# Routed attention with a spectral gate behind it: first row sum in thirds, 64-column similarity and sum products, three-bank transposes, and the first head pair routed first

## The chip, the core and the metric

The kernel runs on one core of a Trainium2 chip. The metric is device time in microseconds, the time of one execution. A profile shows each engine of the core: PE (TensorE, matrix products and transposes), DVE (VectorE), ACT (ScalarE), POOL (GpSimd) and SP (SyncE, which issues transfers). The times of the kernel before are 387.03, 386.67 and 388.61 us; their median is 387.03 us.

## What is computed

The first half is attention with a mask from clusters; q, k and v are (4 batches, 8 heads, 768 positions, 64), and there are 16 centroids for each head. The second half is a projection, a circular convolution along the positions, a gate and an output projection.

```python
q_assign = np.argmax(np.einsum('bhsd,hcd->bhsc', q_n, c_n), axis=-1)      # k_assign likewise
mask = q_assign[:, :, :, None] == k_assign[:, :, None, :]
scores = np.where(mask, scale * np.matmul(q, k.transpose(0, 1, 3, 2)), -1000000000.0)
attn = np.exp(scores - np.max(scores, axis=-1, keepdims=True))
attn = attn / (np.sum(attn, axis=-1, keepdims=True) + 1e-09)              # x = attn @ v
x1, x2, x3 = (proj[..., :D], proj[..., D:2 * D], proj[..., 2 * D:])       # proj = x @ w_proj
x2_conv = np.fft.irfft(np.fft.rfft(x2, n=S, axis=1) * H, n=S, axis=1)     # H = rfft(filter_fft)
y = (x1 * x2_conv * x3) @ w_out
```

## The kernel before

**Pairs and groups.** Two heads make a pair, two pairs a group; there are 16 pairs in 8 groups (n = 0 to 7), and two groups make a batch. A pair goes through six key tiles of 128 positions (sk = 0 to 5). For each key tile there are three score products (L660), three exponentials of 128x512 on ACT (L669, L672), the product of the exponentials with v (L683, 8 recorded matmuls, called "pv" here), and the running sum of the exponentials over the key tiles on DVE (L697): one addition of 128x1536 for each key tile but the first two, which share one (`acc<-p,p`). The sums are later added over the partitions, either by a product with ones on PE (L711; groups 0, 1 and 7) or by transfers that accumulate (L731, issued by POOL; the other groups).

**Routing.** For a group, q and k of both pairs are transposed on PE (L556, for groups 0 and 1 L566), copied out of PSUM by ACT or DVE (L261, L263), multiplied with the normalised centroids (`cbd`) to similarities (L586, for group 0 L477), copied, transposed back (L599), and on DVE the position of the largest of 16 is found and made into mask rows (L607 to L624). A transfer transposes these (L629) and small transfers put 16 mask rows beside each head's q and k (L462), so that the score product adds the mask. The similarity product puts four results of 32 rows each into one bank, each by a product that is 32 columns wide; so does the product with ones.

**Gate.** For every batch, `hyena` computes the projections, the transform, the product with the filter's transform and the way back on PE (L74, L809, L451), with its elementwise work on DVE (L822 to L911). It needs tables of sines (`angles`, L337, with the sine function on ACT) and the filter's transform (`tables`, L375), which the kernel works out once at the start.

**Order of the work.** The kernel writes its instructions in an order that a planner works out (`Plan.place`, L113). Every piece of work is an `op` with a cost for each engine that may do it, a due time, and the buffers it reads and writes. The planner fills the engines' queues by readiness and due time; `NUDGE` shifts single due times, and on PE an op that keeps the array's width (`MODES`, L46) is preferred. Each engine then runs its queue strictly in order. PSUM has six banks for scores and other products (0 to 3, 6, 7) and two for the results of the pv product (4, 5). All of group 0 is routed in the order pair 0, pair 1 while the sines and the tables are worked out between; scores of the first pair follow.

The width of a product counts in what follows. Products whose results are 64 (or 32) rows tall are put two (or four) beside each other on the array; this is the similarity product of a group before:

```python
for z in range(4):
    T.nc.tensor.matmul(bank(h.ids[ch])[64 * (z % 2) + 32 * (z // 2):][:32, :384], T.cbd[:, 2 * g + z // 2],
                       T.qkT[z][:, ch], start=True, stop=True)
```

Of the kernel before, what the change touches and what calls it, by code (L numbers as in the profile page):

```python
# [34 lines left out]
ROWS = 16  # L35
LEAD = 2.99901
FIRST = 2
BUSY = 8.09741
HELD = 4
EARLY = 8.73655  # L40
NUDGE = {6:-0.2,9:0.7,10:3.7,11:-0.3,71:-0.3,75:-1.5,90:7.4,91:7.4,129:-0.8,140:0.4,152:2.6,155:-6.2,156:6.6,158:-2.3,167:0.6,169:-4.1,187:-5.6,193:0.1,204:0.1,207:-0.7,209:0.8,212:-0.2,216:15.5,218:8.0,222:-3.8,228:-3.1,238:-1.7,239:-1.7,240:-1.7,243:1.1,245:-2.9,253:-4.1,255:-7.1,256:-7.1,257:-3.0,264:4.3,274:2.3,281:0.9,288:9.1,289:11.6,298:0.6,322:-4.8,328:-9.2,329:-0.5,343:0.7,363:0.5,368:-1.5,369:-1.5,370:0.7,371:-1.5,375:0.1,378:0.5,379:0.7,390:-1.8,391:-0.1,400:-0.2,406:2.8,409:-4.8,410:0.5,416:0.2,418:-1.0,433:-11.9,434:0.6,440:-3.7,479:0.8,480:-0.3,481:-0.5,485:1.1,494:-0.6,495:-4.2,504:2.3,508:-1.9,511:-0.2,517:-0.3,518:-5.0,523:-0.4,524:0.5,526:2.1,539:-2.3,547:0.2,554:10.5,558:0.3,565:-0.3,568:1.6,573:0.4,587:-4.9,590:0.2,595:-17.3,597:-2.4,617:0.7,620:-1.0,631:0.3,634:2.8,646:0.7,658:0.8,664:0.1,665:-1.9,684:2.2,690:-8.8,693:2.2,698:0.1,703:-7.8,704:-1.7,705:-1.7,729:0.5,740:1.0,750:-0.6,759:0.5,767:0.4,779:-0.7,782:1.7,784:-0.1,788:0.7,789:-0.3,790:0.8,800:2.5,805:-3.5,810:1.5,822:0.1,824:0.1,826:-0.5,828:-0.3,843:-8.5,848:-1.7,861:0.5,870:2.5,871:2.5,872:-1.3,883:-5.3,888:-3.6,897:-0.8,898:-1.1,901:-3.5,915:-3.1,926:4.0,936:-4.1,937:-3.0,940:2.9,941:0.4,947:-0.4,949:-0.6,969:-0.8,981:1.0,996:2.0,997:2.0,999:-0.3,1026:2.7,1029:-2.1,1031:0.1,1036:3.2,1039:2.0,1043:-1.2,1048:1.2,1050:-0.1,1054:-1.5,1056:10.8,1062:0.4,1066:0.9,1077:-7.7,1083:-3.4,1092:-0.1,1098:-1.0,1101:0.3,1116:-6.9,1118:-4.2,1122:2.8,1123:2.4,1124:2.4,1127:1.5,1130:-1.5,1131:0.3,1132:-2.9,1143:-2.6,1150:4.6,1157:-0.6,1194:-0.9,1236:-2.9,1253:-0.5,1255:0.7,1257:0.7,1263:0.3,1270:-0.2,1271:-1.1,1276:-3.6,1285:2.1,1286:4.6,1295:4.9,1311:-2.5,1317:-2.0,1321:0.4,1322:0.7,1332:-1.9,1337:-0.6,1351:5.6,1357:0.2,1359:0.5,1363:-0.5,1373:-1.5,1374:1.1,1381:0.2,1383:-0.3,1414:-2.7,1419:-0.5,1422:0.3,1425:0.7,1441:9.4,1450:3.5,1461:2.0,1478:-1.3,1479:3.3,1500:1.2,1501:-8.3,1521:0.2,1529:0.8,1546:0.2,1551:-0.2,1552:-1.1,1555:1.4,1557:0.1,1563:-0.6,1591:0.2,1600:-0.4,1619:-4.8,1624:2.8,1630:-1.5,1634:0.3,1640:-4.0,1641:-4.0,1642:-13.7,1643:-4.0,1655:-4.1,1657:0.4,1666:0.5,1672:1.9,1677:-0.3,1680:2.8,1681:2.8,1682:2.8,1685:-2.9,1697:-0.5,1713:-7.0,1741:5.6,1747:13.3,1764:1.1,1771:-3.3,1774:3.4,1776:0.2,1788:-7.8,1797:0.1,1808:-0.1,1809:-0.1,1814:-4.0,1817:-2.0,1823:3.3,1827:-0.7,1841:-1.3,1844:0.9,1859:2.4,1862:2.5,1863:2.1,1865:-0.3,1870:-0.4,1887:2.4,1890:3.2,1898:-7.4,1901:-0.8,1902:-1.5,1903:-0.8,1904:-0.8,1905:-1.8,1906:-1.8}
# [4 lines left out]
MODES = {"pv": 64, "bc": 64, "half": 64, "sim": 32, "den": 32, "score": 0, "proj": 0, "inv": 0}  # L46
# [30 lines left out]
class Plan:  # L77
# [6 lines left out]
    def op(self, eng, fn, due, r=(), w=(), alloc=None, free=(), lock=False, byts=0, after=(), kind=None, lat=0.0):  # L84
# [3 lines left out]
        o.seq = len(self.ops)  # L88
        o.due += NUDGE.get(o.seq, 0.0)
# [23 lines left out]
    def place(self, free0, banks_for, switch=0.1, wait=0.1, rate=215e3, bonus=10.84378, margin=0.02195, shape=1.63806):  # L113
# [130 lines left out]
def build(T):  # L244
# [3 lines left out]
    T0 = 20.38450  # L248
    TAU1 = 2.97769
    TAU2 = 3.43320  # L250
    NE = 28
# [26 lines left out]

    def dma(e):
        return (T.nc.scalar if e == "ACT" else T.nc.sync).dma_start  # L280
# [10 lines left out]
    def load_qk(n, pr, j, due, after=()):  # L291
        s = qslot[n, pr, j] = len(loads) % NQK
        loads.append(1)

        return [op({"SP": .8, "ACT": .8} if n == 0 else ("SP", .8), lambda e, hp=hp: dma(e)(
            T.qkraw[s][:, :, hp], (T.q, T.k)[j][n // 2, 4 * (n % 2) + 2 * pr + hp].rearrange(
                "(p t) d -> p t d", t=NT)), due, w=[("qkraw", s, hp)], byts=196e3, kind="load", after=after, lat=.5)
            for hp in range(2)]
# [8 lines left out]
    def centroids():  # L307
# [7 lines left out]
        sq = op(("ACT", 1.5), lambda e: T.nc.scalar.activation(cen.s0, cen.ss, Act.Sqrt), 2.4, r=["ss"], w=["s0"])  # L315
# [13 lines left out]
        def cbd(e):  # L329
            cv = ap(h)[:D, :128].rearrange("d (r e c) -> d r e c", r=4, e=2)  # L330
            V().tensor_copy(T.cbd[:D, :, :NC], cv[:, :, 0])
            V().tensor_copy(T.cbd[D:, :, NC:], cv[:, :, 1])
        op(("DVE", .45), cbd, 2.7, r=[h, "cbd0"], w=["cbd"], free=[h])
        return sq


    def angles(sq):  # L337
        sins = []
        MAGIC = 12582912.0
        sc = 2.0 * math.pi / S  # L340
        for m in range(3):
            lo = 256 * (m // 2)
            n, r = (lambda x=x, m=m, lo=lo: x()[m % 2][:, :, lo:lo + 192] for x in (lambda: T.tm, lambda: T.ob))
            nk, rk = ("tm", m % 2, "a", m), ("ob", m % 2, "a", m)
            kc = lambda: T.kc
            due = 1.9 + .8 * m
# [190 lines left out]
    def routing(n):  # L537
# [39 lines left out]
        if n == 0:  # L577
            return got + first_masks(1)
# [597 lines left out]
```

## Time and profile before

| what | value |
|---|---|
| median of the three times | 387.03 us |
| span of the profiled execution, first to last instruction | 385.4 us |
| first transpose on PE; first score product; first exponential | 5.1; 21.7; 22.4 us |
| ACT copies the first pair's result out (L701) | 42.7 us |
| last exponential starts; last matmul ends | 336.4; 381.0 us |
| exponentials 128x512 on ACT, 288 | 0.61 us each |
| running sum 128x1536 on DVE, 80 | 1.75 us each |
| transfers of 64, 32 and 16 rows that accumulate (L731), 30 | issued by POOL, 0.79 us each |

The profiled execution has no other time of its own than its span; the median of the times is 1.6 us above it, and this is taken for what lies around the span. Busy time of an engine is the time in which at least one of its instructions is recorded. A matmul's record holds its way through the array, so that records of successive matmuls overlap, and their number and mean length do not give the time they need together; the chain of waits, which goes from one start to the next, does.

### The profile page before, as it was taken

How to read it: one execution, taken by the hardware profiler on the slowest of the kernel's cores; microseconds unless marked ns; L12 is line 12 of the kernel's file. 1: busy time of each engine (PE TensorE's matmuls, PEld its weight loads, DVE VectorE, ACT ScalarE, POOL GpSimd, SP SyncE). 2: the span in 40 equal slices, each digit the busy share in tenths (PEclk: the TensorE clock that was granted, in tenths of full speed). 3: DMA queues.
4: the chain of work that ended last, by engine and by line, in shares of the span. 5: the costliest groups of instructions: out<-in, count | busy, mean ns of one | idle time of the engine just before them, and what ended most of it. 6: DMA issues, size and time to landing. Idle time of an engine off the chain costs nothing.

```text
span 385.4 us, 8486 instructions
## 1 busy us (share of the span) xinstructions
PE 367.3 (95%) x3262; PEld 207.6 (54%) x3267; DVE 352.3 (91%) x504; ACT 273.1 (71%) x519; POOL 46.6 (12%) x92
## 2 busy tenths in 40 slices
PE   2999899999999999989999999999999999999995
PEld 1564345445655555556555555555455566555682
DVE  8898988998798999998899999999998999999883
ACT  5897987887894979577975967687867367532342
POOL 8602000000012010101010100101010100000400
PEclk9999999999999999999999999999999999999999
DMA  9819984730679669767886896645657551010214
GB/s 176 196 52 216 215 182 120 170 72 22 166 146 187 119 119 143 121 113 126 161 104 174 144 246 108 119 88 91 102 102 198 62 115 43 4 43 2 101 67 163
DMA packets 93860, 47.17 MB, mean 122 GB/s; under 512 B 82088, under 2 KB 87676, under 8 KB 93820
## 3 DMA queue, kind: packets, MB, share of 16 engines
q1 hardware_dynamic: 87836, 36.84, 42.5%
q0 software_dynamic: 2704, 8.98, 16.0%
q10 hardware_dynamic: 3280, 0.82, 1.2%
q8 instruction: 25, 0.41, 0.5%
q14 instruction: 15, 0.12, 0.1%
HBM read 31.59 MB, written 7.40 MB: 101 GB/s over the span
## 4 chain that ended last, share of the span: by engine, by line
PE 65%; DVE 19%; ACT 6%; issue 4%; DMA 3%; SPq 1%; POOL 0%; DVEq 0%; ACTq 0%; POOLq 0%
PE bank L74 24%; PE pair L683 21%; DVE acc L697 6%; PE bank L809 5%; PE bank L72 4%; PE bank L556 3%; ACT p L672 2%; PE bank L586 2%; DMA dr<-dn 2%; DMA aug<-ohT 2%; ACT aug L261 2%; DVE tm L833 2%; PE bank L599 1%; PE bank L451 1%; PE bank L566 1%
## 5 line engine op out<-in xcount | busy, mean ns | idle before, releaser
L683 PE MATMUL pair<-p,vraw 128*64 128x385 f32 x768 | 142.5, 490 | 0.2
L672 ACT ACTIVATE p<-bank 128x512 f32<-128x512 f32 x192 | 113.7, 613 | 34.1 <-PE bank L74 29.3
L697 DVE TENSOR_TENSOR acc<-p,acc 128x1536 f32<-128x1536 f32 x64 | 112.0, 1750 | 3.9 <-ACT p L672 1.5
L683 PEld LDWEIGHTS pair<-p,vraw 128*64 128x64 f32 x768 | 54.2, 136 | 47.8 <-issue 41.1
L74 PE MATMUL bank<-aug,aug 128*64 128x512 bf16 (+3 forms) x580 | 68.4, 328 | 2.1 <-ACT p L672 1.2
L669 ACT ACTIVATE p<-bank 128x512 f32<-128x512 f32 x96 | 58.6, 611 | 6.2 <-PE bank L74 5.6
L74 PEld LDWEIGHTS <-aug 128*64 128x64 bf16 (+1 forms) x580 | 34.4, 109 | 34.5 <-issue 22.4
L731 POOL DMA_DIRECT2D acc<-acc x30 | 23.6, 788 | 242.6 <-DMA acc<-acc 90.3
L74 PE MATMUL bank<-xT,wpj 128*64 128x384 bf16 x440 | 42.7, 326 | 0.0
L261 ACT COPY qkT<-bank 128x384 f32<-128x384 f32 x63 | 28.1, 497 | 10.5 <-PE bank L74 8.9
L74 PEld LDWEIGHTS <-wpj 128*64 128x64 bf16 x440 | 25.5, 109 | 15.9 <-issue 6.4
L697 DVE TENSOR_TENSOR acc<-p,p 128x1536 f32<-128x1536 f32 x16 | 28.0, 1751 | 3.3 <-ACT p L672 3.1
L74 PEld LDWEIGHTS <-y 128*64 128x64 bf16 x464 | 22.9, 110 | 12.6 <-issue 4.4
L261 ACT CAST aug<-qkT 64x768 bf16<-64x768 f32 x33 | 27.3, 829 | 2.5 <-PE bank L74 1.7
L833 DVE TENSOR_TENSOR tm<-bank,hm 128x512 f32<-128x512 f32 x44 | 27.7, 678 | 0.1
L809 PE MATMUL bank<-wpj,xT 128*64 128x512 bf16 x192 | 21.9, 379 | 0.0
L74 PE MATMUL bank<-wout,y 128*64 128x512 bf16 x176 | 21.1, 379 | 0.0
L72 PE MATMUL bank<-aug,aug 80*128 80x256 bf16 (+3 forms) x92 | 20.0, 321 | 0.2
L556 PE MATMUL bank<-ident,qkraw 128*128 128x128 f32 x144 | 19.6, 279 | 0.3 <-DVE sd L898 0.3
L556 PEld LDWEIGHTS bank<-ident,qkraw 128*128 128x128 f32 x144 | 15.6, 140 | 6.9 <-issue 4.5
L261 ACT COPY tm<-bank 128x512 f32<-128x512 f32 x13 | 7.4, 589 | 15.8 <-PE bank L809 12.0
L701 ACT COPY osb<-pair 128x770 f32<-128x770 f32 x16 | 12.9, 809 | 6.9 <-PE pair L683 6.8
(150 smaller groups left out, 433.0 us busy)
## 6 DMA issues: line engine op xcount, KB each, us to landing
vraw<-in_v_dram SPq DMA_DIRECT2D x16, 384.0 KB, 4.3
qkraw<-in_q_dram SPq DMA_DIRECT2D x30, 192.0 KB, 4.1
qkraw<-in_k_dram SPq DMA_DIRECT2D x30, 192.0 KB, 4.1
rb<-dr SPq DMA_DIRECT2D x30, 192.0 KB, 3.7
out_dram<-ob SPq DMA_DIRECT2D x11, 512.0 KB, 3.0
acc<-acc POOLq DMA_DIRECT2D x10, 384.0 KB, 6.2
acc<-acc POOLq DMA_DIRECT2D x10, 192.0 KB, 4.2
y<-in_moe_filter_fft_dram SPq DMA_DIRECT2D x4, 384.0 KB, 7.1
```

The source lines that it names most:

```text
L72: return T.nc.tensor.matmul(out, lhsT, rhs, start=start, stop=stop)
L74: T.nc.tensor.matmul(out[64 * i:64 * i + 64], lhsT[:, 64 * i:64 * i + 64], rhs, start=start, stop=stop)
L261: T.nc.scalar.copy(out, in_)
L556: T.nc.tensor.transpose(bank(h.ids[i // 3])[:, ts(i % 3, 128)], raw(s, i), T.ident)
L669: T.nc.scalar.activation(o, ap(h).rearrange("p (a b) -> p a b", a=2), Act.Exp, scale=0.125)
L672: T.nc.scalar.activation(flat(s)[:, lo:lo + 512], ap(h), Act.Exp, scale=0.125)
L683: T.nc.tensor.matmul(o[64 * hp:64 * hp + 64, ch, :385], T.vraw[vs][:, hp, sk * D:(sk + 1) * D], T.p[slots[sk]][:, hp, 384 * ch:384 * ch + ...
L697: T.nc.vector.tensor_tensor(T.acc[os], P_(t[0]), P_(t[1]) if len(t) == 2 else T.acc[os], op=Alu.add)
L701: op(("ACT", .83), lambda e: T.nc.scalar.copy(T.osb[o3], two(ob)[:, :, :385]), te, r=[ob], w=[("osb", o3)], free=[ob])
L731: op(("POOL", .8), lambda e, rows=rows: T.nc.gpsimd.dma_start(flat_()[:rows], flat_()[rows:2 * rows], accum_op=Alu.add), te, r=[], w=[("ac ...
L809: T.nc.tensor.matmul(ap(h)[64 * i:64 * i + 64], T.xT[xs][:, kt, c:c + 64], T.wpj[:, kt, DM:2 * DM], start=kt == 0, stop=kt == ND - 1)
L833: op(("DVE", .68), lambda e, i=i, cs=cs, r=r, h=h: T.nc.vector.tensor_tensor(T.tm[r][:, cs], ap(h), hmrow(i, (0, 2, 2, 3)[2 * r + cs]), op ...
```

## The change

- **First sum in thirds.** The addition of the first two key tiles (L697, `acc<-p,p`) becomes three additions of 128x512, each of which follows two exponentials and may run on DVE or POOL. In the order of instructions after the change 26 of the 48 thirds are on DVE and 22 on POOL. The later additions are as before.
- **64 columns.** The similarity product and the product with ones use a 64-column operand padded with zeros, and add two products into one 64-row result. The numbers of matmuls stay (8 calls for a group's similarities, 4 for a sum).
- **Three-bank transposes.** From group 2 on, the 12 transposes of a pair's q and k go to three banks, four to a bank, and are copied by three copies of 128x512 in place of four of 128x384.
- **First pair first.** In group 0, q and k of pair 0 are each routed alone and ahead of pair 1; the sines, the tables and the filter's transform come after the first scores. The function tables for square root and exponential are loaded at the start, and the sines run as one block on ACT in the midst of the first pair. The masks of pair 1 in group 0 go by 8 transfers of 16x384.
- **Around it.** Mask rows and small buffers lie in the similarities' buffer (`sim`). All due times (`NUDGE`) are new, and `ONLY` fixes the engine of 194 ops. On PE the changes of the array's width go from 85 to 53, on DVE there are 506 instructions before and 547 after, on ACT 526 and 492, on POOL 97 and 111, on SP 237 and 243.

```diff
-MODES = {"pv": 64, "bc": 64, "half": 64, "sim": 32, "den": 32, "score": 0, "proj": 0, "inv": 0}
+MODES = {"pv": 64, "bc": 64, "half": 64, "sim": 64, "den": 64, "rows": 32, "score": 0, "proj": 0, "inv": 0}
...
-                for z in range(4):
-                    T.nc.tensor.matmul(bank(h.ids[ch])[64 * (z % 2) + 32 * (z // 2):][:32, :384], T.cbd[:, 2 * g + z // 2],
-                                       T.qkT[z][:, ch], start=True, stop=True)
+                for z in (0, 1, 2, 3):
+                    c, j = z // 2, z % 2
+                    T.nc.tensor.matmul(bank(h.ids[ch])[64 * j:64 * j + 64, :384], T.cbd[:, 2 * g + c, 32 - 32 * c:96 - 32 * c],
+                                       T.qkT[z][:, ch], start=c == 0, stop=c == 1)
...
-                        T.nc.tensor.matmul(ap(h)[32 * z:32 * z + 32, :384], T.ones32, T.acc[os][:, hp, ts(ch, 384)],
-                                           start=True, stop=True)
+                        T.nc.tensor.matmul(ap(h)[64 * hp:64 * hp + 64, :384], T.ones[:, 32 - 32 * ch:96 - 32 * ch], T.acc[os][:, hp, ts(ch, 384)],
+                                           start=ch == 0, stop=ch == 1)
...
+                h = Bank(cls, 3)
+                ss = [qslot[n, pr, x] for x in range(2)]
+                def tr2(e, ss=ss, h=h):
+                    for i in range(2 * NT):
+                        T.nc.tensor.transpose(bank(h.ids[i // 4])[:, ts(i % 4, 128)], raw(ss[i // NT], i % NT), T.ident)
+                for c in range(3):
+                    op(EV512, lambda e, pr=pr, c=c, h=h: copy(e, T.qkP[pr][:, ts(c, 512)], bank(h.ids[c])), due + 1.6,
...
+            if sk == 1:
+                for u in range(3):
+                    def part(e, u=u):
...
+                        alu(e).tensor_tensor(o, x, y, op=Alu.add)
+                    op({"DVE": .63, "POOL": 1.33}, part, due - 1 + .2 * u, r=[("p", slots[i], u) for i in range(2)], w=[("acc", os, u)], lock=True)
+            if sk > 1:
...
+                op(("DVE", 1.75), acc, due + 1.1907 - 40 * (last and sk == NT - 1), r=PK(sk), w=AK, lock=True)
...
+    for z in range(2):
+        load_qk(0, 0, z, .3 + z * .1)
+    load_v(0, 0, 8.0)
+    for z in range(2):
+        load_qk(0, 1, z, 6.5 + z * .1)
+    routing(0)
...
+        attention(n, 0)
+        if n == 0:
+            angles()
+            tables()
```

## The prediction

> **What bounds the kernel now.** I read the page's busy shares first, then busy time by stretch (first score at 21.7 us, first pair's result at 42.7, last matmul ended at 381.0), then the chain of waits.
>
> ```profile
> PE 367.3 (95%) x3262; PEld 207.6 (54%) x3267; DVE 352.3 (91%) x504; ACT 273.1 (71%) x519; POOL 46.6 (12%) x92
> ```
>
> PE leads, DVE is close behind. An average does not tell which of them ends; the stretches do (columns: length, then busy us and count of PE, PEld, DVE, ACT, POOL, then clock and DMA):
>
> ```profile
> 0.00:21.70 21.70, 13.88 (x98) 8.62 (x99) 18.59 (x44) 15.41 (x29) 14.46 (x52) 1.00 0.87 183
> 21.70:43.50 21.80, 20.18 (x161) 10.07 (x160) 20.11 (x31) 18.43 (x37) 2.61 (x5) 1.00 0.76 150
> 43.50:340.10 296.60, 293.08 (x2511) 163.12 (x2515) 278.06 (x372) 224.71 (x428) 24.46 (x31) 1.00 0.63 123
> 340.10:381.00 40.90, 40.16 (x499) 25.81 (x493) 35.49 (x60) 13.94 (x28) 5.08 (x4) 1.00 0.15 57
> ```
>
> PE stands idle 7.8 us before the first score, 1.6 in the first pair, and 3.5 + 0.7 = 4.2 in the 337 us after that. From 43.5 us on the kernel is PE's work one after the other, with a last copy and transfer of 4.4 us. So work added to PE adds to the time, work taken from DVE or ACT returns at most the 4.2 us, and only the head has slack.
>
> **The head has one more loss, the clock.** The page's granted clock is 1.00 throughout, but the chain shows the same transposes at two rates: nine in 1.92 us (213 ns each) at the start, twelve in 1.46 (122 ns with the start) later.
>
> ```profile
> 10.63 1.92 PE bank L566 x9
> 12.55 2.69 PE bank L477 x8
> ...
> 57.58 1.46 PE bank L556 x12
> ```
>
> Up to 14.9 us PE ran at half rate. It was busy 7.7 us by then (4.5 + 2.8 + 0.4), about half of that lost. So the head's slack is 7.8 + 1.6 + 3.9 = 13.3 us, of which 5.1 pass before the first load lands: at most 8.2 us can be won.
>
> Beside these rows, the Trainium skill, "TensorE: Matmul & The Clock Gate", section "Part 1: The HAM clock gate", says that the array starts at half rate and is released after about 3.4 us of sustained work, in a free-running window. The trace agrees as far as it goes: bursts at 5.1 and 7.6 us did not release it, unbroken work from 10.2 us did after some 4.7. By that rule a head with fewer matmuls and more waits stays slow longer, some 1 to 3 us by an estimate from these rows; my sum does not use it.
>
> **Wider products: PE, on the path.** The chain gives what a product costs from start to start (start, us, what):
>
> ```profile
> 102.53 1.30 PE pair L683 x8
> 103.82 0.44 PE bank L74 x6
> 104.26 1.43 PE bank L586 x16
> ...
> 61.36 0.78 PE bank L711 x8
> ```
>
> A pv product (L683) is 64 columns wide: 8 records of 385 columns in 1.30 us, 0.162 us a record. The similarities (L586) are 32 wide: 16 records of 384 columns in 1.43 us, 0.09 a record: twice as many lie beside each other. After the change they are as wide as pv, with the same number of calls, neighbours in the order going to opposite halves, so 16 x 0.162 = 2.60 us: +1.17, seven times, +8.2. The sum product (L711) goes from 0.78 to 8 x 0.162 = 1.30: +0.52, six times, +3.1. In group 0 the two similarities of pair 0 stand alone, one half of the array empty: 0.65 us more each at full rate, +1.3.
>
> What this buys is fewer changes of width, 85 to 53. The chain's 1.43 and 0.78 hold one change each; the 26 at both ends of 13 products leave 13 to count. A price: pv pieces followed by transposes take 1.45 us and others 1.29, so at most 0.16; the 16 records of L586 at 0.081 are 1.30, so 0.13. I take 0.10, as 1.43 also holds the fill: -1.3, and -0.4 for the few other changes. Sum on PE: 8.2 + 3.1 + 1.3 - 1.7 = **+10.9 us** (9 to 13). The transposes stay 12 for a pair whether in two banks a tensor or three a pair: 0.
>
> **The head.** Before the first score PE has 0.5 us less to do by the order of instructions (9.6 against 10.1 at full rate: sines' and group 1's transposes out, 1.3 of similarity in). When does that score come? q's transposes start at 5.1 as before; k's second half landed at 7.6, and the first loads still share the queues with pair 1's: 7.2. Six slow transposes 1.3: 8.5. The two similarities, four calls one after another, 2.6 us at full rate and 5.1 at half: I take 4.3, 12.8. Copy 0.47, transposes 0.4, then ten half-sized DVE operations of some 0.28 us (rows of 0.55): 16.5. Mask transposes, pair 1's similarity and transposes, which PE has ahead of the first score, 1.2 beyond what DVE covers; a copy of 16 rows 0.79: 18.5. That is 3.2 us sooner, 2.7 net of the 0.5. In the first pair ACT is next: from the first exponential to the pair's result it has 26 exponentials (15.9), nine copies (4.5), a cast (0.83), the block of sines with two table loads (6.7, from rows of 1.28, 0.52, 0.62, 0.30, 0.19) and four small copies (1.2): 29.1, less 0.09 of overlap for each of 45, 25.0 us. Before it was 42.7 - 22.4 = 20.3. In that stretch PE has 3.6 us more to do by the order of instructions (20.8 against 17.2: some of it was done later before, 1.2 is the wider similarity), so 4.7 - 3.6 = 1.1 are lost. Head: **-1.6 us**. Bounds: -8.2 (all slack) and +3 (the first score no earlier).
>
> **DVE.** Sixteen additions of 1.751 go: -28.0. 26 thirds of about 0.64 (a 128x512 addition stands at 0.679): +16.6. Copies that go from ACT to DVE by the fixed engines and 512-wide copies: about +15. Net **+3.5** on 352.3; ACT loses 15.5. With PE 98.8% busy after the head neither shows: 0, bounds -4.2 (all idle after the head) and +8 (next part).
>
> **GpSimd.** 22 thirds at 1.28 (the 128x512 addition below) are 28.1 us on an engine that is idle, but it has two snags. It holds up DVE: a DVE operation on one column took 0.78 us beside POOL's 0.82 us cast, its twin before that 0.16. And its queue has L731's transfers, which wait for each other's landing (90.3 us in all for 30), with thirds queued behind; the second addition of the pair on DVE waits for all thirds, and everything behind it on DVE.
>
> ```profile
> 8.46 0.16 DVE L319 TENSOR_TENSOR s<-s,ss 128x1 f32<-128x1 f32 x1
> 8.65 0.78 DVE L320 TENSOR_TENSOR s<-s,s 128x1 f32<-128x1 f32 x1
> ...
> 8.60 0.82 POOL L263 CAST aug<-qkT 64x768 bf16<-64x768 f32 x1
> ...
> L837 POOL TENSOR_TENSOR y<-tm 128x512 bf16<-128x512 f32 x4 | 5.1, 1276 | 50.8 <-DVE tm L833 50.8
> L731 POOL DMA_DIRECT2D acc<-acc x30 | 23.6, 788 | 242.6 <-DMA acc<-acc 90.3 <-DVE acc L697 72.2 <-DVE aug L263 69.8
> ```
>
> DVE's products with a PSUM operand (L833) kept 0.677 us beside L837, so only operations with both inputs in SBUF suffer. Bounds: 0 to 28.1 us of DVE time; I take 4, which DVE's 33 us of idle cover. The Trainium skill, "SBUF — State Buffer", section "SBUF: two separate sides", calls the port pair of the two engines an exclusive lock, held for the whole instruction; the 0.78 us agree. The masks' eight transfers of 16x384 on SP in place of four hide behind pair 0: 0.
>
> **Sum.** 385.4 + 10.9 - 1.6 = 394.7 us of span. Around the span lie 1.6 us (median 387.03 less 385.4): **396.3 us**, 2.4% slower.
>
> **Rivals.**
>
> *DVE becomes the bound through GpSimd.* DVE has 355.8 us to do. If half of the 28.1 us holds it up, 370; with the 33.1 us in which it is idle today, at both ends and waiting for others, 403: 404.6 us. It decides from about 6 us of hold-up (355.8 + 33.1 + 6 = 394.9). For it: nearly all thirds on POOL stand behind a transfer. Against: DVE's idle partly shrinks when it is late.
>
> *The head gives back the price: not slower.* Place: the first 43.5 us. If the first score comes at 12 to 13 us and the pair is not held by ACT, 8.2 us return: 385.4 + 10.9 - 8.2 = 388.1, 389.7 us; with some of the later 4.2 us, 388. It is no slower than 0.5% from about 9 us on. Against: 25 us of ACT work and half rate.
>
> *The wider products cost no more than the narrow ones*, as their number stays: then the width changes return 3.0 (26 at 0.10, and 0.4) and the head 2.9 (1.6, and 1.3 less similarity): 385.4 - 5.9 = 379.5, 381.1 us. Against: pv at 0.162 a record in the same width.
>
> **How the numbers follow.** Forecast 0.65 (391 to 401), GpSimd 0.18 (401 to 407), head 0.12 (386 to 391), narrow price 0.05. The range takes the forecast, most of the GpSimd case and of the head: 387 to 404. 0.5%, about what a measurement of this kernel can tell from no change, is 385.1 to 389.0 us: faster 0.06 (narrow price, a little of the head), same 0.08 (most of the head), slower 0.86.
>
> **What would show it.** Right: similarities near 2.6 us and sum products near 1.3 in the chain; first score at 17 to 20 us; PE over 97% busy after the first pair. Wrong: 16 records in under 1.9 us; a first score before 14 us; PE idle over 10 us after the first pair, with DVE or POOL as releaser (then GpSimd). The forecast also fails if DVE's fewer additions had freed time on PE that these stretches do not show.

## The result, and the profile after

| | before | after |
|---|---|---|
| time, median (range of 4 runs) | 387.11 us (386.67 to 388.61) | 409.77 us (409.22 to 413.07) |
| ratio, 95% interval | | 1.0601 (1.0558 to 1.0644) |
| profiled execution: span, its own time | 385.4 us, 387.0 us | 407.4 us, 409.2 us |
| first score starts | 21.7 us | 18.73 us |
| first pair's result copied | 42.7 us | 44.6 us |
| TensorE busy from 45 us to the last matmul | 331.7 of 336.0 us | 346.4 of 357.4 us |
| TensorE idle in that stretch | 4.25 us | 11.0 us |

The change made the kernel 6.0% slower; the forecast was 2.4%, and the time lies above its range. One of e10's four executions (547.17 us) and one of e12's (411.04 us) fell in a slower state and are left out below. In the changed kernel the line numbers are others: scores L73 and L75 (the products of the gate stand under L75 too), pv L704, similarities L605, sum products L737, three-bank transposes L572, thirds L721, later additions L725, copies L265 (ScalarE) and L267 (VectorE), transposes of the similarities L619, the argmax's comparison L629.

The page's busy shares after:

```profile
PE 381.4 (94%) x3334; PEld 225.6 (55%) x3334; DVE 362.1 (89%) x545; ACT 262.5 (64%) x487; POOL 75.9 (19%) x106
```

TensorE has 14.1 us more than before, VectorE 9.8 more, ScalarE 10.6 less. The busy time by stretch, cut at the first score and at 45 us (columns as in the prediction), with the last stretch of the kernel before as the fourth line:

```profile
0.00:18.73 18.73, 11.44 (x74) 6.99 (x75) 10.42 (x35) 8.88 (x17) 10.79 (x36) 1.00 0.86 169
18.73:45.00 26.27, 23.56 (x171) 13.41 (x171) 24.88 (x48) 23.34 (x50) 3.05 (x10) 0.94 0.79 163
45.00:402.43 357.43, 346.42 (x3092) 205.16 (x3088) 326.82 (x463) 229.18 (x420) 62.06 (x61) 1.00 0.55 108
...
45.00:380.99 335.99, 331.74 (x2998) 188.28 (x2998) 312.05 (x431) 237.15 (x451) 29.54 (x35) 1.00 0.57 115
```

The third line holds the loss: 21.4 us more than before between 45 us and the last matmul, of them 14.7 in which TensorE is busy and 6.8 in which it waits. The second line shows something that the profile of the kernel before does not have between its head and its last matmul: a granted clock below 1. What TensorE waited for, by the waits of the changed kernel (us in total, times, longest):

```profile
...
PE bank L75 <- DMA aug<-sim: 2.6, 2, 1.4
PE bank L403 <- DVE oh L629: 2.2, 1, 2.2
PE bank L572 <- DVE tm L859: 1.9, 1, 1.9
PE bank L75 <- DVE sd L924: 1.4, 2, 1.0
PE bank L75 <- DVE y L937: 1.4, 1, 1.4
PE bank L737 <- DVE acc L725: 1.3, 2, 1.0
...
```

All of these are operations of VectorE, or transfers of masks that VectorE computes. The wait of 2.2 us (L403) lies in the head, at 36.9 us. And the chain of waits shows the products at the prices that were forecast, 2.60 and 1.30 us:

```profile
44.54 1.29 PE bank L737 x8
...
60.97 1.29 PE bank L737 x8
...
104.54 2.58 PE bank L605 x16
...
152.00 2.60 PE bank L605 x16
```

**One stretch shows how the pieces meet.** The timeline of the changed kernel from 138 to 150 us, GpSimd, VectorE, then TensorE (start, us, engine, line, operation; in brackets the idle time before it and its releaser):

```profile
141.38 2.76 POOL L721 TENSOR_TENSOR acc<-p,p 128x512 f32<-128x512 f32 x2
...
141.19 3.96 DVE L267 CAST aug<-qkP 64x768 bf16<-64x768 f32 x2
145.18 0.69 DVE L721 TENSOR_TENSOR acc<-p,p 128x512 f32<-128x512 f32 x1
145.79 2.48 DVE L859 TENSOR_TENSOR tm<-bank,hm 128x512 f32<-128x512 f32 x4
...
142.96 1.46 PE L704 MATMUL pair<-p,vraw 128*64 128x385 f32 x8
...
144.57 0.66 PE L572 MATMUL bank<-ident,qkraw 128*128 128x128 f32 x4
147.13 1.09 PE L572 MATMUL bank<-ident,qkraw 128*128 128x128 f32 x8 [1.90 <-DVE tm L859]
148.15 2.09 PE L704 MATMUL pair<-p,vraw 128*64 128x385 f32 x6
```

Two casts that take 0.57 us each take 3.96 together, as the first, beside two thirds that GpSimd runs in 2.76 us, takes 3.37. The products of L859, queued behind them on VectorE, come late; four of the twelve three-bank transposes are done, the other eight wait 1.90 us, from 145.23 to 147.13 us, for the banks that L859 reads. Then six records of pv take 2.09 us, where eight took 1.46 at 142.96 us: TensorE has lost its clock. The busy time by stretch of the two gaps and of what follows each (the third figure from the end is the clock):

```profile
36.90:39.07 2.17, 0.00 (x0) 0.00 (x0) 2.14 (x6) 0.91 (x2) 0.21 (x3) 1.00 1.04 216
39.07:42.48 3.41, 3.39 (x27) 2.00 (x27) 3.24 (x11) 1.96 (x6) 0.00 (x0) 0.50 0.93 211
144.90:147.00 2.10, 0.33 (x3) 0.09 (x1) 2.07 (x5) 0.95 (x2) 0.77 (x1) 1.00 1.55 198
148.30:151.71 3.41, 3.41 (x16) 1.48 (x16) 3.31 (x2) 0.96 (x3) 0.00 (x0) 0.50 0.87 186
```

### The profile page after: what moved, and what is told of

It reads as the page before. It is cut to its first block, busy times and chain, and to the rows that moved or that the text cites. A ratio compares the mean times of both kernels' runs of the same rounds, so it can differ in the third digit from the quotient of the medians.

```text
span 407.4 us, 8676 instructions
## 1 busy us (share of the span) xinstructions
PE 381.4 (94%) x3334; PEld 225.6 (55%) x3334; DVE 362.1 (89%) x545; ACT 262.5 (64%) x487; POOL 75.9 (19%) x106
## 3 DMA queue, kind: packets, MB, share of 16 engines
q0 software_dynamic: 2704, 8.98, 15.7%
## 4 chain that ended last, share of the span: by engine, by line
PE 53%; DVE 22%; DMA 8%; ACT 6%; issue 4%; SPq 4%; POOL 2%; ACTq 0%; DVEq 0%; POOLq 0%
PE bank L75 20%; PE pair L704 15%; DVE acc L725 5%; PE bank L835 4%; PE bank L605 4%; SPq L473 3%; PE bank L572 3%; DMA aug<-sim 3%; DMA sim<-oh 2%; DVE aug L267 2%; PE bank L737 2%; ACT p L692 2%; DVE tm L859 2%; PE bank L73 2%; DVE x L899 1%
## 5 line engine op out<-in xcount | busy, mean ns | idle before, releaser
L704 PE MATMUL pair<-p,vraw 128*64 128x385 f32 x768 | 144.0, 493 | 0.0
L692 ACT ACTIVATE p<-bank 128x512 f32<-128x512 f32 x192 | 108.7, 605 | 38.9 <-PE bank L75 35.7
L725 DVE TENSOR_TENSOR acc<-p,acc 128x1536 f32<-128x1536 f32 x64 | 112.0, 1750 | 3.5 <-ACT p L692 0.8
L704 PEld LDWEIGHTS pair<-p,vraw 128*64 128x64 f32 x768 | 56.5, 137 | 45.5 <-issue 39.2
L75 PE MATMUL bank<-aug,aug 80*64 80x512 bf16 (+3 forms) x670 | 76.1, 328 | 5.1 <-DMA aug<-sim 2.6
L75 PEld LDWEIGHTS <-aug 128*64 128x64 bf16 (+1 forms) x670 | 42.0, 110 | 41.0 <-issue 26.3
L689 ACT ACTIVATE p<-bank 128x512 f32<-128x512 f32 x96 | 56.9, 604 | 10.1 <-PE bank L75 8.5
L721 POOL TENSOR_TENSOR acc<-p,p 128x512 f32<-128x512 f32 x22 | 33.2, 1557 | 81.1 <-ACT p L692 70.0
L75 PE MATMUL bank<-xT,wpj 128*64 128x384 bf16 x456 | 42.4, 326 | 0.0
L75 PEld LDWEIGHTS <-wpj 128*64 128x64 bf16 x456 | 28.9, 110 | 10.7 <-issue 2.0
L265 ACT COPY qkP<-bank 128x512 f32<-128x512 f32 (+1 forms) x48 | 24.2, 563 | 13.2 <-PE bank L572 6.0
L75 PEld LDWEIGHTS <-y 128*64 128x64 bf16 x480 | 24.4, 110 | 14.1 <-issue 4.2
L859 DVE TENSOR_TENSOR tm<-bank,hm 128x512 f32<-128x512 f32 x44 | 28.0, 683 | 0.9 <-ACT p L689 0.3
L75 PE MATMUL bank<-wout,y 128*64 128x512 bf16 x192 | 23.6, 379 | 1.4 <-DVE y L937 1.4
L265 ACT CAST aug<-qkP 64x768 bf16<-64x768 f32 x28 | 23.1, 829 | 2.2 <-DVE qkP L267 1.7
L265 ACT COPY ob<-bank 128x512 f32<-128x512 f32 x21 | 11.8, 589 | 19.3 <-PE bank L75 18.8
L572 PE MATMUL bank<-ident,qkraw 128*128 128x128 f32 x144 | 18.5, 277 | 1.9 <-DVE tm L859 1.9
L605 PE MATMUL bank<-qkP,cbd 128*64 128x384 f32 x112 | 19.9, 487 | 0.2
L572 PEld LDWEIGHTS bank<-ident,qkraw 128*128 128x128 f32 x144 | 15.6, 141 | 7.7 <-DVE tm L859 2.4
L721 DVE TENSOR_TENSOR acc<-p,p 128x512 f32<-128x512 f32 x26 | 17.8, 692 | 2.0 <-ACT p L692 1.2
```

Of the source, the lines that this page charges most:

```text
L75: T.nc.tensor.matmul(out[64 * i:64 * i + 64], lhsT[:, 64 * i:64 * i + 64], rhs, start=start, stop=stop)
L265: T.nc.scalar.copy(out, in_)
L572: T.nc.tensor.transpose(bank(h.ids[i // 4])[:, ts(i % 4, 128)], raw(ss[i // NT], i % NT), T.ident)
L605: T.nc.tensor.matmul(bank(h.ids[ch])[64 * j:64 * j + 64, :384], T.cbd[:, 2 * g + c, 32 - 32 * c:96 - 32 * c], T.qkT[z][:, ch], start=c == ...
L689: T.nc.scalar.activation(o, ap(h).rearrange("p (a b) -> p a b", a=2), Act.Exp, scale=0.125)
L692: T.nc.scalar.activation(flat(s)[:, lo:lo + 512], ap(h), Act.Exp, scale=0.125)
```

## The experiments

All times are medians, beside runs of the kernel before on the same chip (387.1 to 388.2 us). "Stalls" are TensorE's idle time from 45 us to its last matmul in the profiled execution: 4.25 us before, 11.0 after. As the kernel before itself moves by 1 us from one set of runs to the next, gains are good to about that.

### First question: the width, GpSimd, or the new order?

**e1_narrow**: the changed kernel with the products 32 columns wide again (likewise in group 0), in the changed order.

```diff
-  T.nc.tensor.matmul(bank(h.ids[ch])[64 * j:64 * j + 64, :384], T.cbd[:, 2 * g + c, 32 - 32 * c:96 - 32 * c], T.qkT[z][:, ch], start=c == 0, stop=c == 1)
+  T.nc.tensor.matmul(bank(h.ids[ch])[64 * j + 32 * c:64 * j + 32 * c + 32, :384], T.cbd[:, 2 * g + c, 32:64], T.qkT[z][:, ch], start=True, stop=True)
-  T.nc.tensor.matmul(ap(h)[64 * hp:64 * hp + 64, :384], T.ones[:, 32 - 32 * ch:96 - 32 * ch], T.acc[os][:, hp, ts(ch, 384)], start=ch == 0, stop=ch == 1)
+  T.nc.tensor.matmul(ap(h)[64 * hp + 32 * ch:64 * hp + 32 * ch + 32, :384], T.ones[:, 32:64], T.acc[os][:, hp, ts(ch, 384)], start=True, stop=True)
```

> The changed kernel with the similarity and sum products 32 columns wide again, instructions otherwise in the same places. Theory A (the wide products cost PE their own 10.9 us, and the rest of the loss is GpSimd holding up DVE): the time falls by the products' own price alone, 9.0 + 3.9 + 1.9 for group 0 less 2.6 for the width changes that return, so 397 to 400 us, and PE still stands idle about 11 us between 40 us and its last matmul. Theory B (the order was laid out for products of the narrow price, and the wide ones make the queues meet in the wrong order): the idle goes too, 385 to 390 us.

Measured: 400.31 us, ratio 1.0336 (1.0304 to 1.0369); stalls 12.7 us. It gives 9.5 us back, the products' own price, as theory A has it (the time lies just above its 397 to 400). Theory B falls: the order runs no better with the narrow products.

**e5_before_wide**: the counterpart, the kernel before with the similarities and sum products of groups 1 to 7 made 64 wide, its order unchanged (the edit of the change for L586 and L711; small buffers are put together to make room).

> The kernel before with the similarity product of groups 1 to 7 and the sum product 64 columns wide, order unchanged, small buffers put together to make room. Theory A: only the products' own price, 7 x 1.29 + 6 x 0.64 - 2.6 for 26 width changes = 10.3, so 396 to 399 us with PE idle some 4 to 6 us after the first pair. Theory B: the order was laid out for narrow products here too, so idle of 8 us or more comes on top, 403 to 410 us.

Measured: 395.11 us, 1.0194 (1.0173 to 1.0215); stalls 2.4 us. Its chain has the price of the changed kernel:

```profile
32.42 2.58 PE bank L587 x16
...
62.80 1.29 PE bank L711 x8
```

```profile
45.00:388.99 343.99, 341.60 (x3014) 198.14 (x3008) 313.63 (x431) 238.81 (x454) 29.57 (x35) 1.00 0.56 112
```

So the width costs 8.0 us by itself against the 387.11 of the result (7.3 against the 387.86 beside it), and 9.5 taken back from the changed kernel, which has wide products in group 0 too. The time is a little below the 396 to 399 that theory A gave, and theory B's 403 to 410 are out. In busy time of TensorE after 45 us it is +9.9 (341.6 for 331.7), and 1.9 of that comes back, as TensorE waits 2.4 us in place of 4.25.

**e2_thirds_dve**: GpSimd's 22 thirds done by VectorE at the same places of the order.

```diff
-  alu(e).tensor_tensor(o, x, y, op=Alu.add)
+  T.nc.vector.tensor_tensor(o, x, y, op=Alu.add)
```

> The changed kernel with the 22 thirds of GpSimd done by DVE at the same places of the order. Theory A (GpSimd holds up DVE): the 9.0 us of stretched DVE operations go, with the two half-rate windows on PE behind them; DVE gets 22 x 0.64 = 14 us more work: 402 to 407 us. Theory B (order against wide products): DVE's added work only adds waits, 409 to 414 us.

Measured: 407.26 us, 1.0506 (1.0483 to 1.0528); VectorE 366.3 us busy, stalls 9.1 us. No operation of VectorE is stretched any more. The time lies just above theory A's 402 to 407 and below theory B's 409 to 414.

**e4_no_pool_thirds**: 21 of the 22 thirds on GpSimd are left out, so that the row sums lack them.

```diff
+  if e == "DVE" or (n, pr) == (0, 1):
       alu(e).tensor_tensor(o, x, y, op=Alu.add)
```

> The changed kernel without 21 of GpSimd's 22 thirds: these additions are left out, and DVE does not get them either, so the row sums lack them. It prices all that GpSimd's thirds cost, hold-up and waits. Theory A: 400 to 404 us, no DVE operation stretched, granted clock 1.00 after the head. Theory B: 407 to 410 us, PE idle as before.

Measured: 404.81 us, 1.0441 (1.0398 to 1.0485); VectorE 353.9 us busy, stalls 9.5 us. GpSimd's thirds cost 5.0 us. In the changed kernel eight operations of VectorE take 9.0 us longer than the same operations do elsewhere; here that is 0.2. The time lies between theory A's 400 to 404 and theory B's 407 to 410, and the full clock that theory A expected after the head did not come: 6.83 us at half rate follow from 39.07 us on. With the width this explains some 13 of 22.7 us. Theory A is right as far as it goes, and too small.

### Second question: is VectorE late?

**e7_half_sums** and, as control, **e8_before_half_sums**: the 64 later additions cover only the first head's half (128x768), so that the second head's row sums lack four of six tiles; order unchanged.

```diff
-  T.nc.vector.tensor_tensor(T.acc[os], T.p[slots[sk]][:, :, :S], T.acc[os], op=Alu.add)
+  T.nc.vector.tensor_tensor(T.acc[os][:, :1], T.p[slots[sk]][:, :1, :S], T.acc[os][:, :1], op=Alu.add)
```

> The changed kernel with each of its 64 later row-sum additions cut to half its columns (128x768 for 128x1536), so that the row sums of the second head lack four of six tiles; the order of every queue stays. It takes 64 x about 0.87 = some 56 us from VectorE (362.1 us busy). Of the 22 us that the change added, the wide products explain about 8 (they cost 8.0 added to the kernel before, 9.5 taken from the changed one) and the GpSimd thirds 2.5 to 5. Theory C, for the other 9 to 11: VectorE is late at its appointments, because the new order has given it copies that ScalarE made and filled its queue: with 56 us of slack the stalls of TensorE after the first pair fall from 11.0 us to 4 or less and the time to 394-398. Theory D: the new order itself is at fault (three-bank transposes, mask transfers and loads that come late whatever VectorE does): the stalls stay over 8 us and the time at 402-408.

> The control: the kernel before with the same cut of its 64 later additions (the row sums of the second head lack the same four tiles), order unchanged. Its stalls of TensorE after the first pair are 4.3 us. Theory C: VectorE causes those too, but there are few: 383-386. Theory D: no change, 386-388. If it gains as much as the changed kernel does, VectorE's lateness is no property of the change.

Measured: the changed kernel 396.62 us, 1.0238 (1.0215 to 1.0260), VectorE 313.6 us busy, stalls 4.7; the kernel before 382.51, 0.9886 (0.9866 to 0.9906), VectorE 303.7, stalls 1.8. The same 49 us of relief are worth 13.1 us after the change and 4.6 to 4.9 before it. Theory D's 402 to 408 us are out, and theory C's stalls of 4 or less are missed by little: VectorE's lateness makes most of the stalls. This is the row of the changed kernel so cut:

```profile
45.00:390.46 345.46, 340.76 (x3074) 194.78 (x3070) 279.15 (x462) 226.83 (x417) 58.31 (x58) 1.00 0.56 111
```

Of the 13.1 us, 6.3 are stalls and 5.7 are busy time of TensorE (340.8 for 346.4 us); in this profile the half rate behind the head does not come.

**e9_copies_act**: plain copies out of PSUM that the order gives to VectorE after 45 us are made by ScalarE at the same places. ScalarE made such copies before the change.

```diff
-        o.fn(o.on)
+        o.fn("ACT" if o.on == "DVE" and o.plain and o.start > 45 else o.on)
```

> The changed kernel with the plain copies out of PSUM that VectorE makes after 45 us of the plan (some 28: of the transposed q and k, the similarities, the inverse transforms, tm and x3) made by ScalarE at the same places of the order; casts stay. VectorE is relieved of about 16 us, ScalarE (262.5 us busy of 407.4) gets about 14. Theory C: a part of VectorE's lateness goes: 401-406. Theory D: 407-411. A rival of both: ScalarE's queue, where each copy now waits behind exponentials, makes the copies later than before: 411-416.

Measured: 405.41 us, 1.0467 (1.0420 to 1.0514); VectorE 347.3 us busy, ScalarE 275.6, stalls 10.2. It wins 4.4 us, as theory C has it; the rival that ScalarE becomes the bound falls. The 27 copies that move are more than the change had put on VectorE: its plain copies went from 9.4 to 20.7 us by the change, and this run takes 14.8 us off VectorE.

**e10_narrow_dve_act**: e1, e2 and e9 together.

> The changed kernel with the narrow products, with all thirds on VectorE, and with VectorE's plain copies on ScalarE: what is left of the change is its order, the three-bank transposes, the head, and the split first sum. If the costs add: 400.3 - 2.5 - what the copies are worth (0 to 6) = 392-398. Theory C: 392-395, with stalls after the first pair under 7 us. Theory D: 397-399, as the order's stalls stay. Below 387 it would beat the kernel before, which neither expects.

Measured: 396.29 us, ratio 1.0231 (1.0203 to 1.0260). This lies between theory C's 392 to 395 and theory D's 397 to 399 and decides nothing between them. No version of the changed kernel comes near the kernel before.

### Third question: is it how much VectorE has to do, or where the order puts it?

**e11_replan_wide** and **e12_replan_narrow**: the order laid out anew, with the planner's prices set to measured ones and other shifts of due times (`NUDGE`) and engines (`ONLY`). Some of the prices are shown; e12 has the narrow products and keeps the first two as they were.

```diff
-op(("PE", 1.33), sim, b0,
+op(("PE", 2.6), sim, b0,
...
-op(("PE", .68), den, te + 0.5,
+op(("PE", 1.29), den, te + 0.5,
...
-op({"DVE": .63, "POOL": 1.33}, part, due - 1 + .2 * u,
+op({"DVE": .70, "POOL": 1.56}, part, due - 1 + .2 * u,
```

> The changed kernel with its order laid out anew: the planner's prices are set to what the traces show (similarity product 2.6 us for 1.33, sum product 1.29 for 0.68, cast on VectorE 0.58 for 0.50, largest-of-sixteen 1.1 for 0.85, its multiplication 0.66 for 0.56, gather of the row sums 0.85 for 0.50, third on VectorE 0.70 for 0.63 and on GpSimd 1.56 for 1.33), and the table of shifts of due times and the choices of engine are sought anew for these prices; the instructions are the same but for the engine of some copies. Theory E: the open 8 to 10 us are appointments missed because the order of the changed kernel was laid out to the microsecond for prices that the chip does not keep: with this order the stalls of TensorE after the first pair fall from 11.0 us to 6 or less and the time to 398-404, while the wide products keep their 8 to 9. Theory D, that the three-bank transposes and the split first sum make the stalls by what they are: 406-411, stalls over 9 us.

> The same new layout for the changed kernel with the narrow products (their planned 1.33 and 0.68 stay, as the chip keeps them; the other prices as measured), against 400.3 us for the narrow products in the order of the change. Theory E: 386-393, about 10 below the run in the old order and 9 to 12 below the wide one; it could come out level with the kernel before or a little under. Theory D: 396-401.

Measured: wide 409.99 us, 1.0553 (1.0494 to 1.0612), stalls 10.7; narrow 405.95, 1.0433 (1.0347 to 1.0519), stalls 14.0. Theory E falls: better prices for these operations do not give an order that keeps its appointments. The wide run lies in theory D's range; the narrow one is above both (386 to 393 and 396 to 401) and 5.6 us slower than the narrow products in the old order (e1). Two other orders with VectorE at 359 to 362 us stall as much as the first or more.

**e13_before_dve11**: the kernel before, in its own order, with one operation more on VectorE in each pair, which changes no value.

```diff
   T.nc.vector.tensor_tensor(T.acc[os], P_(t[0]), P_(t[1]) if len(t) == 2 else T.acc[os], op=Alu.add)
+  if t == (3,):
+      x = T.acc[os][:].rearrange("p a b -> p (a b)")[:, :512]
+      T.nc.vector.tensor_tensor(x, x, x, op=Alu.max)
```

> The kernel before, in its own order, with one operation more on VectorE in each of the 16 pairs: after the addition of the fourth tile the first 128x512 of the row sums are replaced by their maximum with themselves, which changes no value (about 0.69 us each by the thirds of the changed kernel, 11 us in all). VectorE then has some 363 us of work, as it has in the changed kernel (362.1). Theory F: VectorE's load by itself makes the open stalls, as it stands at 92% of the time already: stalls of TensorE after the first pair rise from 4.3 us to 9 or more, time 393-398. Theory G: it is not how much VectorE has to do but where the order puts it, and the order of the kernel before has room: 387-390.

Measured: 395.71 us, 1.0215 (1.0150 to 1.0279). The page's shares, and the row of the busy time by stretch from 45 us to the last matmul:

```profile
PE 368.2 (94%) x3262; PEld 207.3 (53%) x3267; DVE 362.8 (92%) x520; ACT 273.2 (69%) x519; POOL 46.7 (12%) x92
```

```profile
45.00:388.83 343.83, 332.19 (x2984) 187.34 (x2984) 321.67 (x445) 236.26 (x449) 29.58 (x35) 1.00 0.56 112
```

VectorE has 10.5 us more than before and the kernel takes 8.2 us more (395.71 less the 387.54 beside it). TensorE has as much to do as before (332.2 and 331.7 us), and stands idle 343.83 - 332.19 = 11.6 us, as in the changed kernel (11.0). The shares of the chain of waits say it too, with 30% on VectorE where it was 19%:

```profile
PE 55%; DVE 30%; issue 8%; ACT 6%; DVEq 0%; POOL 0%; POOLq 0%; ACTq 0%
```

This is the clearest run of the study: nothing of the change is in it but VectorE's load. Theory F holds, theory G falls. The added operation stands at one place of each pair, in the running sum; what it would cost at another place is not shown.

**e14_before_thirds**: the kernel before with its first additions split in thirds, 20 of 48 on GpSimd (`o`, `x` and `y` are a third of the sums and of the two tiles, as in the changed kernel).

```diff
-  T.nc.vector.tensor_tensor(T.acc[os], P_(t[0]), P_(t[1]) if len(t) == 2 else T.acc[os], op=Alu.add)
+  for u in range(3):
...
+      (T.nc.gpsimd if u == 0 or (u == 1 and n % 4 == 1) else T.nc.vector).tensor_tensor(o, x, y, op=Alu.add)
```

> The kernel before, in its own order, with its first addition of each pair split into the thirds of the changed kernel, at the place of that addition: 20 of the 48 thirds on GpSimd (the first of each pair, the middle one of every second pair of groups), 28 on VectorE. VectorE's own work falls by 28.0 - 19.4 = 8.6 us, but its next addition waits for GpSimd, and its casts are held up beside it. Theory A's share for GpSimd (2.5 to 5 us in the changed kernel): 388-393, with some 9 us of stretched operations on VectorE. If GpSimd's thirds only cost where the order is tight: 386-388.

Measured: 391.60 us, 1.0103 (1.0048 to 1.0158); stalls 7.6 us. Giving VectorE's work to an idle engine makes the kernel 4.1 us slower: VectorE's busy time rises by 3.4 us (355.7) although it has 8.6 less to do, so that it is held up for some 12 us. One of the places, VectorE and GpSimd in the timeline:

```profile
174.65 2.67 DVE L263 CAST aug<-qkT 64x768 bf16<-64x768 f32 x3
...
175.05 1.29 POOL L707 TENSOR_TENSOR acc<-p,p 128x512 f32<-128x512 f32 x1 [2.84 <-ACT p L672]
```

Three casts take 2.67 us; at 0.574 each they would take 1.7. The missing 1.0 us is one cast, which starts at 175.12 us and takes 1.63, held while GpSimd adds.

### Fourth question: what is left when VectorE is relieved?

**e15_no_masks**: the mask transfers of groups 2 to 7 are left out, so that the scores there use old masks and wait for no routing. **e16_light_dve**: e4 and e9 together. **e17_light_no_masks**: all three.

```diff
+  if n > 1:
+      return
   if n:
       return dma(e)(o, T.ohT[64 * j + 2 * pr + hp:64 * j + 64:4])
```

> The changed kernel without the mask transfers of groups 2 to 7: the mask rows of those groups keep what groups 0 and 1 left there, so that the scores wait for no routing chain, and SyncE's queue waits for no transposing transfer; all compute instructions stay. Theory H, late masks: the 2.6 us of waits for them and the queueing behind them go, 402-406. Theory F, VectorE alone: what the masks held up waits for VectorE next: 407-410.

> The changed kernel without 21 of GpSimd's 22 thirds (the row sums lack them) and with VectorE's plain copies on ScalarE: both reliefs together, VectorE at some 339 us. Alone they gave 5.0 and 4.4 us. Theory F: they add, 399-402, stalls after the first pair 6-8 us. Theory H: the masks and loads are late whatever VectorE does, 403-405.

> Both: VectorE at some 339 us and no mask transfers in groups 2 to 7 (21 thirds and the masks of those groups are left out). Theory F: as without the first, 399-402. Theory H: 396-399. If both are needed: below either by 3 us or more. The floor that the wide products set is 395.1, the time of the kernel before with wide products.

Measured: e15 406.75 us, 1.0503 (1.0463 to 1.0543), stalls 9.4; e16 401.39, 1.0380 (1.0336 to 1.0425), VectorE 337.0, stalls 5.2; e17 398.13, 1.0276 (1.0234 to 1.0318), stalls 5.1. The two reliefs of VectorE add (5.0 and 4.4 alone, 8.4 together), as theory F has it. Leaving out the masks wins 3.0 us alone (406.75, between theory H's 402 to 406 and theory F's 407 to 410) and 3.3 beside the reliefs. The profiles of e16 and e17 cannot show where: the two profiled executions took nearly the same time, 400.42 us, the fastest of e16's four, and 400.19, the slowest of e17's. The kernel before was not run without its masks, for which its TensorE waits 0.4 us.

**e18_filler** and **e19_light_filler**: 20 matmuls that nobody reads, in TensorE's gap at 36.6 us, in the changed kernel and in e16.

```diff
   T.nc.tensor.transpose(bank(h.ids[i // 3])[:, ts(i % 3, 128)], T.sim[:, i // 3, ts(i % 3, 128)], T.ident)
+  for i in range(20 if n == 1 else 0):
+      T.nc.tensor.matmul(bank(h.ids[1])[:, 384:], T.identb, T.identb, start=True, stop=True)
```

> The changed kernel with 20 matmuls more that nobody reads (128 columns in bf16, identity by identity, into columns of a bank that nothing uses) right after the six transposes of group 1's similarities, where TensorE waits 2.2 us for VectorE; by the transposes of the tables they take about 0.055 us each, some 1.1 us, and end before VectorE does, so that nothing waits for them. Theory K, idle time takes the clock: the gap is cut to about 1.2 us, the half rate at 39 us does not come, and the time falls by 1.5 to 3.5 us (407 or so). Rival L: the half rate comes from something else (VectorE's or the transfers' activity there), and stays: 409-411.

> The same filler in the kernel with both reliefs of VectorE (401.4 us, half rate for 6.8 us behind the same gap; 21 thirds left out). Theory K: 397.5-400, no half rate before the end. Rival L: 401-402.

Measured: e18 404.68 us (two executions at 402.8, two at 406.5), 1.0424 (1.0350 to 1.0498); e19 398.77, 1.0260 (1.0192 to 1.0329). More work on TensorE makes the kernel faster by 5.1 and 2.6 us, the first more than the 1.5 to 3.5 that theory K gave. The busy time by stretch of e18, for the rest of the gap, what follows it, and the whole:

```profile
36.60:37.92 1.32, 0.21 (x4) 0.11 (x2) 1.32 (x4) 0.00 (x0) 0.00 (x0) 1.00 1.06 235
37.92:42.48 4.56, 3.58 (x36) 1.85 (x36) 4.39 (x12) 3.22 (x9) 0.00 (x0) 1.00 0.61 138
0.00:396.07 396.07, 377.90 (x3352) 226.47 (x3354) 360.12 (x545) 260.91 (x485) 75.88 (x106) 1.00 0.57 116
```

In this execution the clock stays at its full rate to the last matmul. Theory K's mechanism holds here and rival L falls, but the filler is no sure cure: the mean clock of e18's four executions is 1.0, 0.998, 0.989 and 0.995 (0.984 to 0.992 in the changed kernel), and the profile of e19 still has half rate for 6.83 us from 40.4 us on, which theory K had ruled out.

**e20_all_out**: e17 and the filler.

> The changed kernel with all that helped, but with the wide products: plain copies on ScalarE, 21 thirds and the masks of groups 2 to 7 left out, and the 20 matmuls nobody reads behind group 1's similarities. If the pieces add: 401.4 - 3.3 - 2.6 = 395.5, level with the kernel before with wide products (395.1), and nothing of the change is left unexplained but its width. If masks and filler won the same time: 398.

Measured: 396.69 us, 1.0226 (1.0196 to 1.0255; that is 395.1 to 397.4 us, with 395.5 in it and 398 outside). The pieces add but for 1.2 us; 1.6 us separate it from the kernel before with wide products.

## Why the prediction was wrong

**The step that failed** is the one on VectorE and GpSimd: "With PE 98.8% busy after the head neither shows: 0", and "I take 4, which DVE's 33 us of idle cover". I read idle time of VectorE as cover, and work on it as free up to that amount. It is far from free: 10.5 us more on VectorE, in the old order and with no other edit, cost 8.2 us (e13), some 0.8 us for each. VectorE is a second bound. In the kernel before it is idle for 335.99 - 312.05 = 23.9 us between 45 us and the last matmul, by the list of its waits some 9 us for results of ScalarE and some 8 for results of TensorE; e13 shows that work added there hardly fits in. Relief works less well: 49 us less gave the kernel before only 4.6 to 4.9 (e8). The kernel before stood at the knee, where load costs and relief brings little, and a profile of one kernel shows only the second side (4.2 us of TensorE's idle to be won).

**By the steps of the sum:**

- *Width, +8.2 and +3.1, less the saved changes of width*: right. 2.58 to 2.60 and 1.29 us were forecast as 2.60 and 1.30. The whole without group 0, 9.6, came to 9.9 us of TensorE's time and 8.0 us of the kernel's (e5). The rival that the wide products cost no more falls.
- *Head, -1.6*: right in its times, but the gain is not shown. The first score came at 18.73 us (forecast 18.5), the first pair's result at 44.6, about 2 us later than before (by the forecast's terms 18.5 + 0.7 + 25.0 = 44.2). But the head left a gap of 2.2 us at 36.9 us, in which VectorE makes three casts ahead of the argmax, and this gap cost the clock. Counting TensorE's busy time half where the clock was half (an estimate from the records), the changed kernel had done 30.3 us of work by 45 us and the kernel before 31.9: it was not ahead. The slower start that the prediction thought of, 1 to 3 us, did not come either: the full rate began at 11.76 us, before the change at 15.11 (8.8 to 12.1 and 12.8 to 15.7 in the runs made from them).
- *The clock*: not in the sum at all. Two stretches of 3.41 us at half rate lose 3.4 us by themselves; the filler, which removes the first of them and shortens the gap, won 5.1 us (2.6 with VectorE light).
- *VectorE, 0*: wrong, as above. Its net of +3.5 became +9.8. Of that, 9.0 are operations held up beside GpSimd. Taking its plain copies away wins 4.4 us (e9).
- *GpSimd, 4 us of hold-up, covered*: mis-sized, 9.0 in place of 4, and not covered: 5.0 us of time (e4), and 4.1 where the split is put into the old order (e14). The reading that only operations with both inputs in SBUF suffer was wrong too: the longest hold-up is that of a cast, which has one input. The kernel before had such a place, with two casts at 1.69 us (0.57 each elsewhere) beside one on GpSimd:

```profile
13.18 1.69 DVE L263 CAST aug<-qkT 64x768 bf16<-64x768 f32 x2
...
13.33 1.13 POOL L263 CAST aug<-qkT 64x768 bf16<-64x768 f32 x1
```

Of the rivals, the one on GpSimd reckoned with half of GpSimd's 28 us as hold-up, 14 us; the 9.0 lie halfway between that and the 4 that I took. Its time, 404.6 us, is nearer than the forecast, and its mechanism is there, but it makes 5 us of the 22.7: without GpSimd's thirds the kernel still takes 404.8. The rival that the head gives the price back falls with the first score, which came at 18.73 us and not at 12 to 13.

**The account**, in the order of the runs: 387.1 us before; +8.0 for the width (395.1, e5; 7.3 beside its own runs of the kernel before); +1.6 not told apart (396.7, e20; the wider similarities of group 0, which e5 leaves narrow, are in it); +1.4 for the gap in the head and its clock (398.1, e17; it is 2.6 between e19 and e16); +3.3 for the masks (401.4, e16); +8.4 for VectorE's load, that is GpSimd's thirds and the copies (409.8). The last three are what it wins to take a thing out of the changed kernel, and not exact shares of the change: e16 leaves VectorE 337.0 us of work, 15 less than the kernel before has, and the kernel before has masks too. Shown are the width, VectorE's load and GpSimd's hold-up, each from both kernels, and that the pieces add. Not shown is which of the three-bank transposes, the new due times and the split first sum makes the order stall more than the old one at the same load: with VectorE at 347 to 354 us the changed kernel stalls 9.5 to 10.2 us (e4, e9), the kernel before 4.25 at 352. Taking the three-bank transposes out alone would have moved every other instruction, and was not tried.

Two rules of the Trainium skill bear on this. "SBUF — State Buffer", section "SBUF: two separate sides", says that GpSimd and a VectorE operation with two SBUF inputs or in a fast mode lock each other out for a whole instruction. The trace agrees (the cast of 3.37 us beside 2.76 us of thirds, 0.574 alone); I had read this rule and still put the hold-up at a seventh of GpSimd's 28 us. "TensorE: Matmul & The Clock Gate", section "HAM oscillation — how this bites in real kernels", gives as rule that no idle gap should be longer than about 3.4 us. Here the trace disagrees: gaps of 2.2 and 1.9 us were followed by half rate, and the measurement decides.

## What to carry to other kernels

When two engines are both busy for nine tenths of the time, the idle time of the second need not be cover: before counting an operation on it as free, add a neutral operation to the old kernel and measure the slope (here 8.2 us for 10.5). Work moved from a busy engine to an idle one can hold the busy one up and cost more than it saves (e14). A gap of two microseconds on TensorE can be paid twice, once as a gap and once at half rate behind it.

## What the runs showed of the hardware

- **The clock goes in steps of 3.413 us.** In the clock records the full-rate stretches last 27.307, 105.813, 256.000 and 368.639 us (8, 31, 75 and 108 times 3.413) and the half-rate ones 3.413 or 6.827. In the changed kernel a gap ended the full rate at the end of the step in which it fell: the gap that ended at 39.09 us brought half rate from 39.07, the one that ended at 147.13 from 148.30. Gaps of 2.07 us (e13, at 165.6 us) and 2.52 us (e11, at 209.5), each of which lies across the border of two steps, cost no clock. How much idle time a step bears, the runs don't settle: e17 kept the clock through a step with a gap of 1.75 us (at 56.5), and e19 lost it behind a gap of 1.1.
- **A third on GpSimd is no bargain.** 128x512 took 1.56 us there on average (1.27 at least) and 0.69 on VectorE. Beside it, casts, products out of SBUF and even an operation on 12 columns (1.97 us in place of 0.17) stood still; none of the eight stretched operations of the changed kernel reads PSUM.
